# Two more zero fills with 8 KB rows while the zero buffer is half lent out

## The chip, the cores and the metric

One core of a Trainium2 chip. The metric is device time in microseconds of one execution; lower is better. A program on one core has no second state that could be seen here: all runs quoted are of the fast state, and they are compared only with runs of the kernel before from the same rounds on the same chip.

## The reference, cut to what matters

The reference is one decode step of a transformer block (attention over a window of a KV cache, then a gated FFN) with its backward pass. Only the shapes of the gradients matter:

```python
Hkv, Sk, Dh = 8, 32768, 256
W = min(4096, max(256, Sk // 4))          # 4096: only the last 4096 positions are attended to
k = jnp.repeat(k_cache[:, :, Sk - W:, :], rep, axis=1)
v = jnp.repeat(v_cache[:, :, Sk - W:, :], rep, axis=1)
# outputs 2 and 3: gradients of k_cache and v_cache, bfloat16 [1, 8, 32768, 256] each
```

Seven eighths of both cache gradients are zeros that must be written: some 235 MB out of the 281 MB that the kernel writes.

## The kernel before: the parts that matter

The zeros come from a zero buffer of 16 KB in each of the 128 partitions of SBUF, the core's on-chip memory (`ZW` = 8192 bf16 values). A **fill** writes 2.10 MB from it. Most fills use rows of 16 KB, the whole width, up to four fills in one issue. In the FFN stage SBUF is short, and the upper half of the zero buffer holds the weights of FFN block 1. Meanwhile fills are sent "in halves": rows of 8 KB, read twice from the lower half.

```python
HALF0, HALF1 = 42, 55      # fills 42..54 go out in halves
zeros = ar(0, ZW)
wgu_off = [RB + 28 * KB, ZW // 2]   # block 1's gate and up weights: upper half of the zero buffer

def send_fills(n0, n1, halves=False):
    ...
            if halves:
                for r in range(n):
                    ZQ.dma_start(out=reg[r].rearrange("p (k f) -> p k f", k=2),          # L138
                                 in_=zeros[:, 0:ZW // 2].unsqueeze(1).to_broadcast([128, 2, ZW // 2]))
            elif n == 1:
                ZQ.dma_start(out=reg[0], in_=zeros)                                      # L140
            else:
                ZQ.dma_start(out=reg.rearrange("n p f -> p n f"), in_=...)               # L142
    ...
send_fills(0, HALF0)
send_fills(HALF0, HALF1, True)
...
for n in range(len(BLOCKS)):                                    # three FFN blocks
    ...
    nc.vector.tensor_copy(out=gu_f[:, :, cs], in_=gu_ps[:, :, 0:nb])                     # L421
    ...
    for c in range(4):                                          # last use of the block's weights
        ...
        nc.vector.tensor_tensor_reduce(out=wc, in0=wc, in1=dgb[0:kp, 0:2 * w], ...)      # L438
    if n + 2 < len(BLOCKS):
        load_block(n + 2)
    if n == 1:
        nc.vector.memset(ar(ZW // 2, ZW // 2), 0.0)                                      # L443
        send_fills(HALF1, len(fills) - 1)
```

`ZQ` is GpSimd's queue; loads and other stores are issued by SyncE and ScalarE. The order of instructions on each engine, and the waits, are set by a scheduler.

## Time and profile before

| | before |
|---|---|
| median of the timed runs | 796.41 us (795.74 to 797.07) |
| busy: PE, VectorE, ScalarE | 59%, 52%, 25% of the span |
| moved by DMA | 334.75 MB, mean 420 GB/s |
| rate over 380 to 390 us | 261 GB/s |

Two lines set the scale: the table of queues (packets, MB, share of the time of the 16 DMA engines):

```profile
q0 software_dynamic: 15824, 216.01, 64.0%
q1 hardware_dynamic: 11382, 116.68, 34.9%
```

GpSimd's fills (q0) are two thirds of all bytes. They go to one queue with up to eight issues in flight, and fill every gap that the other transfers leave, as long as that queue holds something.

### The profile page before, as it was taken

Reading aid. Unit: us, or ns where it says so; the run is one execution under the profiler, and the core shown is the slowest. Engines: PE = TensorE matmul, PEld = TensorE weight load, DVE = VectorE, ACT = ScalarE, POOL = GpSimd, SP = SyncE. Lnnn points to the kernel's source line nnn. Section 1 sums busy time; section 2 is a strip of 40 time slices with the busy share of each in tenths; the row PEclk is TensorE's granted clock in tenths of the full one; section 3 lists DMA queues with packets and bytes.
Section 4 is the critical chain, followed back from the end, with each engine's and each line's share of the span. In section 5 each row is a group of like instructions: output and inputs, shape, how many; then the busy total and the mean of one; then the engine's idle time right before and its main releaser. Section 6 shows DMA issues by size and latency. Waiting matters only on the chain.

```text
span 796.7 us, 7253 instructions
## 1 busy us (share of the span) xinstructions
PE 470.7 (59%) x2926; PEld 218.9 (27%) x2926; DVE 410.4 (52%) x621; ACT 196.0 (25%) x309; POOL 35.4 (4%) x52
## 2 busy tenths in 40 slices
PE   0359998999999999353227658583450553361000
PEld 0233433344343433141116524241110211130000
DVE  2106673846648475152883488377661584472200
ACT  0043223142240301000101217372330343162200
POOL 5000000000000000100300000000000000010000
PEclk9988999999999999755557969796565556685555
DMA  9999999999999999999899999999999999999997
GB/s 349 429 431 429 429 431 430 429 430 431 429 429 430 424 425 423 416 421 422 349 421 406 429 428 428 430 431 428 426 425 432 424 429 427 427 422 410 428 443 327
DMA packets 28680, 334.75 MB, mean 420 GB/s; under 512 B 2143, under 2 KB 5223, under 8 KB 7143
## 3 DMA queue, kind: packets, MB, share of 16 engines
q0 software_dynamic: 15824, 216.01, 64.0%
q1 hardware_dynamic: 11382, 116.68, 34.9%
q10 hardware_dynamic: 1440, 1.61, 0.6%
q8 instruction: 23, 0.38, 0.2%
q14 instruction: 11, 0.08, 0.0%
HBM read 53.69 MB, written 280.59 MB: 420 GB/s over the span
## 4 chain that ended last, share of the span: by engine, by line
another core or an unknown queue 36%; DMA 29%; DVE 14%; PE 9%; issue 2%; POOL 1%; ACT 1%; DVEq 0%; ACTq 0%; SPq 0%; POOLq 0%
DMA out_dram<-arena 29%; DVE arena L469 2%; DVE arena L658 2%; DVE arena L554 2%; PE rows_ps L266 2%; PE dqb_ps L512 2%; DVE arena L659 2%; PE d_ps L651 2%; PE tr_ps L263 1%; DVE arena L524 1%; DVE arena L438 1%; POOL out_dram L138 1%; PE dqb_ps L515 1%; DVE arena L623 1%
## 5 line engine op out<-in xcount | busy, mean ns | idle before, releaser
L322 DVE TENSOR_TENSOR arena<-arena,p_f 128x2048 bf16<-128x2048 bf16 x64 | 145.3, 2286 | 64.9 <-PE M_ps L327 64.8
L327 PE MATMUL M_ps<-arena 128*128 128x512 bf16 x512 | 129.6, 382 | 0.2 <-ACT arena L333 0.2
L651 PE MATMUL d_ps<-arena 32*128 32x512 bf16 x256 | 44.8, 507 | 104.8 <-DVE arena L659 90.3
L263 PE MATMUL tr_ps<-ident_bf,arena 128*128 128x128 bf16 x1024 | 90.6, 238 | 20.0 <-DMA arena<-in_A_k_cache_dram 12.3
L266 PE MATMUL rows_ps<-arena,vpad 128*16 128x512 bf16 x256 | 87.3, 436 | 22.1 <-DVE arena L623 16.1
L263 PEld LDWEIGHTS <-arena 128*128 128x128 bf16 x1024 | 67.0, 106 | 72.8 <-issue 59.2
L280 ACT COPY arena<-tr_ps 128x1024 bf16<-128x1024 bf16 x64 | 61.8, 1016 | 69.9 <-PE tr_ps L263 69.9
L330 PE MATMUL ok_ps<-arena 128*16 128x512 bf16 x256 | 63.8, 381 | 0.9 <-DVE arena L307 0.9
L655 ACT CAST arena<-d_ps 128x512 bf16<-128x512 f32 x64 | 37.7, 588 | 103.4 <-PE d_ps L651 103.4
L327 PEld LDWEIGHTS <-arena 128*128 128x128 bf16 x512 | 43.4, 99 | 59.2 <-issue 23.5
L621 ACT COPY arena<-tr_ps 128x1024 bf16<-128x1024 bf16 x32 | 32.5, 1016 | 108.1 <-PE tr_ps L263 48.3
L659 DVE CAST arena<-d_ps 128x512 bf16<-128x512 f32 x64 | 43.5, 679 | 20.8 <-DMA out_dram<-arena 20.8
L658 DVE CAST arena<-d_ps 128x512 bf16<-128x512 f32 x64 | 43.8, 684 | 16.1 <-PE d_ps L651 15.6
L651 PEld LDWEIGHTS <-arena 32*128 32x128 bf16 x256 | 10.6, 95 | 129.9 <-issue 80.0
L656 ACT CAST arena<-d_ps 128x512 bf16<-128x512 f32 x64 | 38.2, 596 | 22.0 <-DMA out_dram<-arena 22.0
L266 PEld LDWEIGHTS <-vpad 128*16 128x16 bf16 x256 | 18.7, 91 | 57.7 <-issue 49.5
L330 PEld LDWEIGHTS <-arena 128*16 128x16 bf16 x256 | 19.1, 89 | 41.5 <-issue 20.4
L142 POOL DMA_DIRECT2D out_dram<-arena x25 | 19.3, 775 | 230.3 <-DMA out_dram<-arena 230.2
L549 DVE TENSOR_SCALAR arena<-arena,xT 128x1792 bf16<-128x1792 bf16 (+1 forms) x9 | 7.7, 881 | 35.5 <-DMA out_dram<-arena 35.5
L295 ACT ACTIVATE e_f<-cols_ps,nbias 128x32 f32<-128x32 f32 x16 | 4.5, 285 | 86.8 <-DVE nbias L291 86.8
L524 DVE CUSTOM_DVE_ANT_0 arena<-arena 128x4096 bf16<-128x4096 bf16 x3 | 13.1, 4423 | 23.2 <-ACT arena L517 23.2
L268 DVE COPY arena<-rows_ps 16x512 f32<-16x512 f32 x16 | 10.8, 676 | 27.5 <-PE rows_ps L266 27.5
(199 smaller groups left out, 388.6 us busy)
## 6 DMA issues: line engine op xcount, KB each, us to landing
out_dram<-arena POOLq DMA_DIRECT2D x13, 8192.0 KB, 167.9
out_dram<-arena POOLq DMA_DIRECT2D x12, 6144.0 KB, 171.5
out_dram<-arena SPq DMA_DIRECT2D x18, 2048.0 KB, 26.7
out_dram<-arena POOLq DMA_DIRECT2D x14, 2048.0 KB, 59.6
arena<-in_A_v_cache_dram SPq DMA_DIRECT2D x10, 2048.0 KB, 52.7
arena<-in_A_k_cache_dram SPq DMA_DIRECT2D x8, 2048.0 KB, 31.9
out_dram<-arena SPq DMA_DIRECT2D x4, 4096.0 KB, 29.9
arena<-in_A_wq_dram SPq DMA_DIRECT2D x2, 3072.0 KB, 21.3
```

The lines of the kernel that those rows point to most:

```text
L263: nc.tensor.transpose(tr_ps[:, dh, i, :], X_sb[:, 4 * q + i, dh * 128:(dh + 1) * 128], ident_bf[:])
L266: nc.tensor.matmul(rows_ps[:], lhsT=pad[:, dh, 16 * q:16 * q + 16], rhs=XT[:, dh].rearrange("p t k -> p (t k)"), start=(q == 0 and dh == 0 ...
L280: sT_ps = dots(kv_at(K_off[g]), KT_slot, vpad[g % 2], rows1, ps_c, "cols", lambda q, XT, ps: nc.scalar.copy(out=XT, in_=ps))
L322: nc.vector.tensor_tensor(out=pK, in0=K_sb[:, 4 * c:4 * c + 4, :].unsqueeze(2).to_broadcast([128, 4, 2, Dh]), in1=p_f[:, c::8, :].unsqueez ...
L327: nc.tensor.matmul(M_ps[:, vh, :], lhsT=V_sb[:, t, vh * 128:(vh + 1) * 128], rhs=pK[:, i, :, :].rearrange("p h d -> p (h d)"), start=(t == ...
L330: nc.tensor.matmul(ok_ps[:].rearrange("p k d -> p (k d)"), lhsT=ppad[g % 2][:, 8 * (t % 4) + t // 4, :], rhs=both(g, t), start=(g == 0 and ...
L621: nc.scalar.copy(out=XT, in_=ps)
L651: nc.tensor.matmul(d_ps[:, qi].rearrange("p w d -> p (w d)"), lhsT=rTm[32 * q:32 * (q + 1), l, :], rhs=R_sb[32 * q:32 * (q + 1), :], start ...
L655: nc.scalar.copy(out=stV[:, t:t + 2, :], in_=d_ps[:, :, 0, :])
L656: nc.scalar.copy(out=stK[:, t:t + 2, :], in_=d_ps[:, :, 1, :])
L658: nc.vector.tensor_copy(out=stV[:, t:t + 2, :], in_=d_ps[:, :, 0, :])
L659: nc.vector.tensor_copy(out=stK[:, t:t + 2, :], in_=d_ps[:, :, 1, :])
```

## The change

The intent: send two more fills in halves, so that GpSimd's queue holds work until the upper half of the zero buffer is zero again.

```diff
-HALF0, HALF1 = 42, 55
+HALF0, HALF1 = 42, 57
```

## The prediction

> **What bounds the kernel now.** I read four views, from coarse to fine. The page first, for the busy shares of the engines and the row of DMA rates:
>
> ```profile
> PE 470.7 (59%) x2926; PEld 218.9 (27%) x2926; DVE 410.4 (52%) x621; ACT 196.0 (25%) x309; POOL 35.4 (4%) x52
> ...
> DMA  9999999999999999999899999999999999999997
> GB/s 349 429 431 429 429 431 430 429 430 431 429 429 430 424 425 423 416 421 422 349 421 406 429 428 428 430 431 428 426 425 432 424 429 427 427 422 410 428 443 327
> ```
>
> No compute engine is above 59% of the 796.7 us, and the DMA engines are at nine tenths or more in 38 of 40 slices. 334.75 MB moved at some 428 GB/s would take 782 us by itself, so the transfers are the bound and the only time to be had is time in which they stand still. Each slice is 19.9 us. The low ones are the first (start), the last (drain) and one in the middle: slice 20, 378 to 398 us, with 349 GB/s. The second view, the windows, shows that place more finely. The columns are the stretch, its length, busy time and count of PE, PEld, DVE, ACT and POOL, the granted clock, the DMA share and GB/s:
>
> ```profile
> 364.00:380.00 16.00, 3.66 (x40) 3.19 (x40) 3.53 (x6) 0.00 (x0) 0.00 (x0) 0.50 1.02 424
> ...
> 380.00:382.00 2.00, 0.00 (x0) 0.00 (x0) 1.58 (x6) 0.00 (x0) 0.00 (x0) 0.50 0.63 262
> 382.00:384.00 2.00, 0.00 (x0) 0.00 (x0) 2.00 (x4) 0.00 (x0) 0.15 (x1) 0.50 0.11 45
> 384.00:386.00 2.00, 1.82 (x5) 0.46 (x5) 1.93 (x9) 0.00 (x0) 2.00 (x4) 0.50 0.63 270
> ...
> 380.00:390.00 10.00, 4.17 (x23) 2.53 (x24) 8.20 (x22) 1.01 (x1) 5.86 (x8) 0.50 0.67 261
> ...
> 390.00:410.00 20.00, 5.11 (x18) 3.51 (x16) 14.59 (x42) 1.51 (x4) 0.74 (x1) 0.50 1.02 431
> ```
>
> The DMA engines are nearly idle around 383 us. Over 380 to 390 us they moved 261 GB/s, where the 20 us after moved 431: (431 - 261) / 431 x 10 us = 3.9 us of lost transfer time. The third view, GpSimd in order of time, names the cause. L138 sends the fills with 8 KB rows, which read the lower half of the zero buffer alone; L140 and L142 send fills with 16 KB rows, which need both halves:
>
> ```profile
> 333.92 0.66 POOL L138 DMA_DIRECT2D out_dram<-arena  x1 [6.37 <-DMA out_dram<-arena]
> 340.11 0.67 POOL L138 DMA_DIRECT2D out_dram<-arena  x1 [5.53 <-DMA out_dram<-arena]
> 383.85 0.55 POOL L140 DMA_DIRECT2D out_dram<-arena  x1 [43.07 <-DVE arena L443]
> 384.39 5.32 POOL L142 DMA_DIRECT2D out_dram<-arena  x7
> ```
>
> The thirteenth small-row fill goes out at 340.11 us. GpSimd then stands 43.07 us, until VectorE has zeroed the upper half again (L443). Eight fills can be in flight (the issues come singly after the first eight), so at 340.11 us some eight fills of 2.10 MB were queued: 16.8 MB, or 39.6 us at 424 GB/s, ending near 380 us. That is where the rate falls. The fourth view, VectorE in order of time, says why the zeroing is not earlier:
>
> ```profile
> 376.10 0.17 DVE L421 COPY gu_f<-gu_ps 128x10 f32<-128x10 f32 x1 [13.75 <-PE gu_ps L420]
> 376.64 1.22 DVE L438 CUSTOM_DVE_ANT_0 arena<-arena 128x1024 bf16<-128x1024 bf16 x1 [0.37 <-DMA out_dram<-arena]
> ...
> 381.79 1.76 DVE L443 MEMSET arena<- 128x2048 uint32 x1 [0.41 <-DVE hh_f L424]
> ```
>
> VectorE runs its program in order, and the copy that belongs to FFN block 2 stands ahead of the last use of block 1 (L438), after which alone the upper half is free. That copy waited 13.75 us for matmuls, which waited for block 2's weights (issued at 355.7 to 357.6 us, landing up to 17.8 us later). The zeroing ends at 383.55 us. The chain of waits puts 42.70 us before L438 down to a store; I don't read that as a dependence on the last small-row fill, since L438 starts while those fills are still moving.
>
> **What the Trainium skill says.** "DMA: Bandwidth & Descriptors", section "Issuing engines are not separate DMA queues": transfers of all issuing engines run on the same 16 DMA engines and interleave. The trace agrees: fills from GpSimd and loads from SyncE together give 420 GB/s from 340 to 364 us, no more than fills alone. The same page, section "Queues, rings and completion order": each DMA engine goes round its rings packet by packet. So two fills queued behind other fills in the same ring delay no weight load, only what follows in that ring. The queue table is in keeping with long packets (216.01 MB in 15824 packets, 13.7 KB each); the turn-taking itself I can't see in it. The same page, section "Why small descriptors are slow (HBM only)", states about 3 cycles of overhead per packet and one cycle per 32 bytes. As an estimate from that page, a row of 16 KB takes 512 + 3 and two of 8 KB take 512 + 6, 0.6% more. The trace has 424 GB/s where small-row fills dominate (364 to 380 us) and 431 with 16 KB rows (390 to 410 us), 1.7% apart, so that is what I use.
>
> **The change part by part.** The order of the instructions on PE, VectorE, ScalarE and SyncE, waits included, is the same in both kernels but for buffer numbers. On GpSimd the 13 small-row issues become 15, the one single 16 KB-row fill (L140) goes and the next group of three (L142) becomes one of two. Bytes stay the same.
> - Added: two issues at 0.67 us each on GpSimd, in its 43 us wait. Cost 0. They go out as soon as two older fills have landed; the last small-row fills went out 5 to 10 us apart, so about 346 and 352 us.
> - Added to the queue: 2 x 2.10 = 4.19 MB, 9.9 us at 424 GB/s. The queue that ran dry at about 381 us now lasts to about 391 us.
> - Unmoved: the zeroing, ending at 383.55 us. Block 2's loads are in other rings, and the fill ring was full until 380 us before too, so they land as before. The 16 KB-row fills go out at 383.9 us as before, now some 7 us before the ring runs dry instead of 3 us after; their start-up lies beside the tail of the small rows.
> - Gain: 3.9 us of lost transfer time. Cost of the smaller rows: 4.19 MB at 424 instead of 431 GB/s, 9.88 - 9.72 = 0.2 us. Removed: one issue of 0.55 us, which was part of the hole already counted.
> - Sum: -3.9 + 0.2 = -3.7 us.
>
> Does it reach the end? In every 10 us window from 400 to 780 us the DMA share is 0.99 or more. GpSimd's fills end about 3.7 us sooner, SyncE's stores then have the engines to themselves sooner, and VectorE's late waits (12.05 us before 729.42) are for stores. SyncE issues its last block of stores and fills from 743.5 us on: 18.9 MB. From there to the end 20.9 MB were moved, so 2.1 MB, 4.9 us, were still queued. Even if no computation came earlier, a lead of 3.7 us fits into that queue, with 1.2 us to spare. So 796.4 - 3.7 = 792.7 us, 0.5% less.
>
> **The rivals.**
> - *The small-row fills hold up the zeroing.* L438 waits on the landing counters of all eight fill slots. If it counted the last small-row fills, two more would move it by up to 9.9 us and the hole would come back at 391 us: some 796 to 797 us, perhaps more with the FFN late. Against it: it ran at 376.64 us, and even the quickest landing of a small-row fill (45.9 us) puts the thirteenth at 386 us.
> - *The computation sets the end, and the hole was hidden.* Then nothing changes: 796 us. For it: the queue behind the last computation is only 4.9 us deep, and less than a start-up can open a new hole, of perhaps 1 us. Against it: the DMA share, and that the late computation itself waits for stores.
> - *Small rows cost more than I take.* The stretches of 412 GB/s in the FFN phase, if they were due to the fills and not to the small weight loads beside them, give 4.19 MB / 412 = 10.2 us, 0.5 us more than now: 793.1 us.
> - *A reshuffle downstream.* All stores after 384 us meet other packets; a wait can fall luckily or not by 1 to 2 us either way.
>
> **Range and chances.** The central sum is 792.7 us. The three times before spread over 1.3 us, the reshuffle gives 1 to 2 us either way, and half of the gain may be lost late: 790.8 to 795.4 us. Over 2% is 15.9 us, four times the hole, and there is no other hole of that size; a loss of that size needs a new wait in every later stage. Faster 0.01, same 0.98, slower 0.01.
>
> **What would show it.** In the profile after: fifteen L138 issues, the last near 352 us; GpSimd's wait for L443 about 12 us shorter; L443 still at about 381.8 us (right) or near 391 us (first rival right); the rate over 380 to 390 us at 420 GB/s or more instead of 261 (hole closed); the last 16 KB-row group and SyncE's last stores some 3 to 4 us earlier (lead kept), or a new low window after 690 us (second rival). I am wrong if the zeroing moves, or if the hole closes and the span stays.

## The result, and the profile after

Median 793.54 us (792.95 to 793.97, 4 runs), against 796.63 us (795.74 to 797.07, 4 runs) for the kernel before in the same rounds. Ratio 0.9962, with a 95% interval of 0.9945 to 0.9979: 3.1 us less, within 2%. (Ratios here are the mean time of one kernel's runs over that of the other's of the same rounds, so not quite the ratio of the medians quoted.)

First the page of the changed kernel, the rows of the DMA share and rate in 40 slices of 19.8 us:

```profile
DMA  9999999999999999999999999999999999999997
GB/s 346 429 431 430 429 431 430 430 430 429 432 429 427 428 426 421 415 422 421 430 434 422 424 430 429 429 424 432 426 425 429 427 426 432 432 419 407 415 435 336
```

The 349 GB/s in slice 20 is gone (430 now); only the first and last slices stay low. The same place in windows:

```profile
364.00:380.00 16.00, 3.69 (x40) 3.19 (x40) 3.62 (x8) 0.04 (x1) 0.00 (x0) 0.50 1.02 425
380.00:390.00 10.00, 4.26 (x23) 2.52 (x24) 8.11 (x22) 1.02 (x2) 4.48 (x6) 0.50 1.01 428
390.00:410.00 20.00, 5.01 (x18) 3.51 (x16) 14.67 (x42) 1.50 (x4) 1.53 (x2) 0.50 1.01 433
```

The last column is to be read: 428 GB/s over 380 to 390 us instead of 261. GpSimd in order of time shows the added issues:

```profile
340.15 0.67 POOL L138 DMA_DIRECT2D out_dram<-arena  x1 [5.49 <-DMA out_dram<-arena]
346.14 0.66 POOL L138 DMA_DIRECT2D out_dram<-arena  x1 [5.32 <-DMA out_dram<-arena]
351.85 0.67 POOL L138 DMA_DIRECT2D out_dram<-arena  x1 [5.04 <-DMA out_dram<-arena]
383.77 4.48 POOL L142 DMA_DIRECT2D out_dram<-arena  x6 [31.25 <-DVE arena L443]
```

The issues at 346.14 and 351.85 us are the two new ones, each as soon as an older fill had landed. GpSimd now waits 31.25 us for the zeroing instead of 43.07, and only six issues go out at once, because two of the eight places in flight are still taken by small-row fills: the queue has not run dry. VectorE in the same place:

```profile
376.01 0.17 DVE L421 COPY gu_f<-gu_ps 128x10 f32<-128x10 f32 x1 [13.14 <-PE gu_ps L420]
...
381.71 1.76 DVE L443 MEMSET arena<- 128x2048 uint32 x1 [0.42 <-DVE hh_f L424]
```

Nothing moved: the zeroing starts at 381.71 us, before it was 381.79. The end of the kernel, from SyncE's queue in order of time, first before, then after (L661 issues the last blocks of gradients):

```profile
715.85 7.74 SPq L661 DMA_DIRECT2D out_dram<-arena  x2
743.53 1.62 SPq L661 DMA_DIRECT2D out_dram<-arena  x2
```

```profile
719.00 3.17 SPq L661 DMA_DIRECT2D out_dram<-arena  x2
742.52 1.57 SPq L661 DMA_DIRECT2D out_dram<-arena  x2
```

The computation that feeds these stores is not 3 us earlier: one pair is 3.2 us later, the last pair 1.0 us earlier. The gain is not in the computation but in the queue of transfers. From 742.52 us on 18.87 MB were issued and, by the trace, 19.45 MB moved, so some 0.6 MB (1.3 us) was still queued at that moment, against 2.1 MB (4.9 us) before. That is 3.6 us less queue with the last stores 1.0 us earlier, and 4.6 us together: the span of this profile is 4.5 us shorter (796.7 to 792.2 us).

### The profile page after: what moved, and what is told of

It reads as the page before. It is cut to its first block, busy times and chain, and to the rows that moved or that the text cites. A ratio compares the mean times of both kernels' runs of the same rounds, so it can differ in the third digit from the quotient of the medians.

```text
span 792.2 us, 7254 instructions
## 1 busy us (share of the span) xinstructions
PE 472.8 (60%) x2926; PEld 220.0 (28%) x2926; DVE 410.6 (52%) x621; ACT 195.9 (25%) x309; POOL 36.2 (5%) x53
## 3 DMA queue, kind: packets, MB, share of 16 engines
q0 software_dynamic: 16096, 216.01, 64.1%
## 4 chain that ended last, share of the span: by engine, by line
another core or an unknown queue 36%; DMA 29%; DVE 14%; PE 9%; issue 2%; POOL 1%; ACT 1%; DVEq 0%; ACTq 0%; SPq 0%; POOLq 0%
DMA out_dram<-arena 29%; DVE arena L469 2%; DVE arena L658 2%; PE rows_ps L266 2%; DVE arena L554 2%; PE dqb_ps L512 2%; DVE arena L659 2%; PE d_ps L651 2%; PE tr_ps L263 1%; DVE arena L524 1%; DVE arena L438 1%; PE dqb_ps L515 1%; POOL out_dram L138 1%; ACT arena L621 1%
## 5 line engine op out<-in xcount | busy, mean ns | idle before, releaser
L266 PE MATMUL rows_ps<-arena,vpad 128*16 128x512 bf16 x256 | 89.0, 443 | 22.0 <-DVE arena L623 15.9
```

Source lines behind the costliest of these rows:

```text
L266: nc.tensor.matmul(rows_ps[:], lhsT=pad[:, dh, 16 * q:16 * q + 16], rhs=XT[:, dh].rearrange("p t k -> p (t k)"), start=(q == 0 and dh == 0 ...
```

## The experiments

**Theory.** The transfers alone set the end. What the change saves is one hole in them, between the last small-row fill and the zeroing, and the zeroing is late because VectorE's order puts a copy that needs block 2's weights ahead of block 1's last use. **Rivals:** the gain comes from the number of small rows; the zeroing waits for the small-row fills; the late computation sets the end, or soon will.

Eight kernels ran, in two sets of four, on two chips; each set has its own runs of the kernel before (medians 796.53 us of 11 runs and 796.83 us of 9).

### h53, h56, h57: fewer fills in halves, one more, and the change again

```diff
-HALF0, HALF1 = 42, 55
+HALF0, HALF1 = 42, 53      # h53;  42, 56 in h56;  42, 57 in h57
```

> Eleven small-row fills. Theory (the transfer hole is the whole effect): two fills of 2.10 MB less, 9.9 us at 424 GB/s, are queued when the zeroing still ends near 383 us, so the fills run dry near 371 us and the hole grows from 3.9 to some 13.7 us: 796.6 + 9.7 = 806.3 us (804.5 to 807). Rival (the end is set by computation, the hole is partly hidden): clearly less than 803 us.

> Fourteen small-row fills. Theory (hole): one more fill adds 4.9 us of queue, the fills would run dry near 386 us, after the 16 KB-row fills are issued at 383.9 us; the hole is closed but for about half a us of start-up: 793.1 to 793.8 us, the same as with fifteen. Rival (the gain goes with the number of small rows): half of the gain of fifteen, 795.1 us.

> The changed kernel again, beside the others: 793.5 us, 0.996 of before. Also a second profile of it: if the late computation near 715 us is again 1 to 3 us later than before, that lateness belongs to the change; if not, it is scatter.

| kernel | fills in halves | GB/s, 380 to 390 us | median us | ratio to before (95%) |
|---|---|---|---|---|
| h53 | 11 | 274 | 807.17 | 1.0134 (1.0115 to 1.0152) |
| before | 13 | 261 | 796.53 | 1 |
| h56 | 14 | 423 | 793.70 | 0.9967 (0.9953 to 0.9981) |
| h57 | 15 | 428 | 793.30 | 0.9961 (0.9945 to 0.9976) |

In h53 the hole starts earlier. Its windows over 364 to 380 and 380 to 390 us:

```profile
364.00:380.00 16.00, 3.65 (x40) 3.18 (x40) 4.91 (x10) 0.00 (x0) 0.00 (x0) 0.50 0.50 208
380.00:390.00 10.00, 4.97 (x25) 2.63 (x25) 7.65 (x18) 1.80 (x4) 6.12 (x8) 0.50 0.69 274
```

The engines do half their work over 16 us: (425 - 208) / 425 x 16 + (431 - 274) / 431 x 10 = 11.8 us lost. The expectation was 13.7. The zeroing ended at 381.84 us instead of 383.55, so the hole was shorter than I had taken. Of these 1.7 us, 1.3 were there already when block 2's weights were issued (354.37 us instead of 355.71); h61 and h85 below issue them as early and never run dry, so the hole is not the reason, and what is stays open. Between the two profiled executions the sum closes: the hole grew by 11.8 - 3.9 = 7.9 us and the span by 8.2 us (796.7 to 804.9). Between the medians the time rose by 10.7 us, against 9.7 expected: the profiled execution of the kernel before was a slow one (798.43 us; see the sum in "Why the prediction was right"), and the five runs of h53 spread over 3.4 us.

The response is the one of a hole, not of a count: two fills fewer cost 10.7 us, one more gains 2.8, two more gain 3.2. One fill (4.9 us of queue) covers a hole of 3.9 us; the second finds next to nothing left to cover. The rival that goes by the number of small rows expected 795.1 us for h56 and falls.

### early: the zeroing earlier, with thirteen fills in halves as before

```diff
-            nc.vector.tensor_copy(out=gu_f[:, :, cs], in_=gu_ps[:, :, 0:nb])
+            with (tc.issue_after(zeroed.ins) if n == 2 else ExitStack()):
+                nc.vector.tensor_copy(out=gu_f[:, :, cs], in_=gu_ps[:, :, 0:nb])
 ...
-                nc.vector.memset(ar(ZW // 2, ZW // 2), 0.0)
+                zeroed = nc.vector.memset(ar(ZW // 2, ZW // 2), 0.0)
```

This only queues block 2's copy behind the zeroing on VectorE. (Two other tries gave no run: a buffer of its own for block 1's weights, which did not fit, and a higher priority for L438, which left VectorE's order as it was.)

> Thirteen small-row fills as before, but block 2's first copy on VectorE is queued behind the zeroing of the upper half, so that block 1's last use and the zeroing no longer wait for block 2's weights. Theory (the late zeroing makes the hole, and it is late by VectorE's order alone): zeroing ends near 371 us instead of 383.5, the 16 KB-row fills are queued before the small ones run out, the rate over 380 to 390 us is 420 GB/s or more, and the time is 792.5 to 793.7 us without any added small row. Rival (the zeroing waits for the small-row fills, or the added rows themselves help): zeroing stays near 382 us and the time 796.6 us.

Median 793.59 us, ratio 0.9962 (0.9948 to 0.9976). VectorE's zeroing and block 2's copy (L444 and L422 in this file), GpSimd's next issue and the window, from three views of this run:

```profile
369.06 1.76 DVE L444 MEMSET arena<- 128x2048 uint32 x1 [0.49 <-DVE dhn L439]
...
376.59 0.17 DVE L422 COPY gu_f<-gu_ps 128x10 f32<-128x10 f32 x1 [5.28 <-PE gu_ps L420]
```

```profile
371.12 0.55 POOL L140 DMA_DIRECT2D out_dram<-arena  x1 [30.66 <-DMA arena<-in_B_w_gate_dram]
```

```profile
380.00:390.00 10.00, 3.42 (x23) 2.38 (x22) 8.37 (x14) 2.42 (x5) 1.54 (x2) 0.67 1.03 440
```

The zeroing ends at 370.82 us, 12.7 us sooner, and the hole is closed (440 GB/s) without one added small row. (The profile puts GpSimd's wait down to a weight load that landed about then; the issue follows the end of the zeroing by 0.30 us, as in the kernel before.) So VectorE's order made the zeroing late, and neither the small-row fills nor their count. The last stores are issued at 732.24 us, 11.3 us sooner than before, with 4.5 MB (10.5 us) still queued instead of 0.6 MB, and the time is that of the changed kernel. Computation that is 10 us ahead buys nothing.

### h61 and h85: many more fills in halves

```diff
-HALF0, HALF1 = 42, 55
+HALF0, HALF1 = 42, 61      # h61;  42, 85 in h85
```

> Nineteen small-row fills. Theory (hole): the hole is closed with fourteen, so four more than in the changed kernel gain nothing; their rows cost 8.4 MB at 424 instead of 431 GB/s, 0.3 us: 793.3 to 794.2 us. Rival (small rows help by themselves): 3 us less per two fills, below 790 us.

> Forty-three small-row fills, 28 more than in the changed kernel (58.7 MB). If the 1.7% between 424 and 431 GB/s belongs to the rows, they cost 58.7/424 - 58.7/431 = 2.2 us: 795.6 us; if only 0.6% does, 0.8 us: 794.2 us. If rings take turns by packet, loads that run beside 8 KB rows instead of 16 KB rows get more of the engines: the 3 MB weight load issued near 420 us lands in some 20 to 23 us instead of 28.6.

h61 (nineteen): median 794.20 us, ratio 0.9960 (0.9946 to 0.9975), no more gain than with fourteen. h85 (forty-three): 796.40 us, ratio 0.9989 (0.9974 to 1.0004). The difference of the two ratios, 0.0029, is 2.3 us (from the scatter of the five runs each, 1.0 to 3.4 us) for 24 more fills, 50.3 MB: in rows of 8 KB these bytes take some 2% longer than in rows of 16 KB (2.3 of 118.6 us at 424 GB/s). The 1.7% that the prediction took from two windows lies inside these bounds. That includes all else that the rows bring about. By the windows h85 falls 1.0 MB (2.3 us) behind h61 between 390 and 580 us, about where it alone still sends 8 KB rows (until some 600 us), and no further after that. Enough of them eat most of the gain.

In h85 other loads run beside 8 KB rows instead of 16 KB ones. The 3 MB load of L471, from issue to landing, first in h57, then in h85:

```profile
DMA to landing us min/median/max: 29.0/29.0/29.0
```

```profile
DMA to landing us min/median/max: 22.1/22.1/22.1
```

It lands 6.9 us sooner; in all nine kernels but h85 it takes 27.8 to 29.9 us. That is in keeping with rings (the lists of waiting transfers, one for each queue on each DMA engine) that take turns by packet ("DMA: Bandwidth & Descriptors", section "Queues, rings and completion order"), if a packet is a row. The page doesn't say that it is (it speaks of several descriptors to a packet), and no run here isolates the turn-taking. The gradients' last stores then go out much earlier:

```profile
719.21 4.12 SPq L661 DMA_DIRECT2D out_dram<-arena  x2
```

That is 23 us ahead of h57 (742.54 us), and the kernel is 2 to 3 us slower. This shows most clearly that the computation is not what is waited for.

### h57m2 and earlym2: two fills left out

Both kernels leave 4.19 MB of one output unwritten and are wrong for it (that output compares as NaN). All else stays.

```diff
-                send_fills(HALF1, len(fills) - 1)
+                send_fills(HALF1, len(fills) - 3)    # in h57 for h57m2, in early for earlym2
```

> The changed kernel with two 16 KB-row fills of the last group left out (wrong result on purpose: 4.19 MB of the output stay unwritten). If the transfers alone set the end, 4.19 MB at 430 GB/s go: 793.4 - 9.8 = 783.6 us. Rival (only some 2 us of queue are left behind the last computation, and the computation does not come earlier): 789 to 792 us, with a new low window near 735 to 745 us.

> The kernel with the early zeroing, with the same two fills left out (wrong result on purpose). Its computation runs some 10 us ahead of the changed kernel's, so both theories expect the whole 9.8 us here: 783.8 us. If it gains no more than the changed kernel without the two fills, the late computation is not what holds that one.

h57m2: median 783.47 us, ratio 0.9830 (0.9815 to 0.9844). earlym2: 783.75 us, ratio 0.9832 (0.9818 to 0.9846). Both lose the whole 9.8 us to be had for 4.19 MB. The rival, that the changed kernel has only some 2 us before the late computation binds, falls. The reason is VectorE's wait late in the kernel, in h57 and then in h57m2:

```profile
728.43 0.69 DVE L659 CAST arena<-d_ps 128x512 bf16<-128x512 f32 x1 [9.80 <-DMA out_dram<-arena]
```

```profile
719.16 0.69 DVE L659 CAST arena<-d_ps 128x512 bf16<-128x512 f32 x1 [1.73 <-DMA out_dram<-arena]
```

The wait is for a store to free a buffer. When transfers are ahead, it shrinks, and the last stores follow (733.28 us instead of 742.54). Of it 1.73 us are left, and the handover to the last stores begins to show: from 732 to 734 us the DMA share is 0.60 in h57m2. How the time goes on beyond that was not tried.

No version beats the changed kernel clearly: h56, h57, h61 and early all lie between 793.3 and 794.2 us.

## Why the prediction was right, point by point

- **The hole and its size.** Right in cause: the rate over 380 to 390 us went from 261 to 428 GB/s, and closing the hole in another way (early) gave the same time. That the estimate of the queue (16.8 MB, 39.6 us, dry near 380 us) came out right was partly luck: by the packets in the trace 14.9 MB of small rows were left to send after 340.11 us, not 16.8, and 2.5 MB of other transfers shared the engines, which together is about as long (41 us).
- **The added fills cost nothing to issue and go out near 346 and 352 us.** Measured: 346.14 and 351.85 us. GpSimd's wait was to shorten by about 12 us: 11.8.
- **The zeroing does not move.** Right, 0.08 us apart; the first rival falls.
- **The sum, -3.7 us.** Measured -3.1 us, with an interval of 1.7 to 4.4 us less. The direction and mechanism held, and 3.7 lies inside the interval. The four kernels that close the hole gain 2.6 to 3.2 us, early too, which adds no small rows, so the 0.2 us of small rows is not the term that is off. The hole was measured in one profiled execution, which took 798.43 us, above all four timed runs of before beside it (795.74 to 797.07; in the later sets 798.87 is reached). Between the two profiles the span fell by 4.5 us, between the medians by 3.1. Part of this can be seen: from 420 to 430 us that execution moved 377 GB/s, where the other kernels, h85 (391) left out, moved 410 to 426; that is some 0.9 us. That the hole, too, is smaller in a usual execution is possible, but no profile shows it. (A slip in the third rival's sum: 10.2 us in place of 9.88 gives 793.0, not 793.1.)
- **The lead reaches the end.** Right: by the bytes moved, the changed kernel is ahead of the kernel before by 1.7 MB at 390 us, 2.3 MB at 430 us and still 1.9 MB (4.4 us) at 780 us. In the details half right: GpSimd's last 16 KB-row group went out 3.2 us earlier (500.04 instead of 503.22), but SyncE's last stores only 1.0 us earlier where I had 3 to 4, and those before them 1.1 to 3.2 us later. The fallback in the same step held: most of the lead went out of the 4.9 us of queue and left 1.3. What makes the middle stores some 1 us later is open (h57 has it too: 674.46 us for the pair that stood at 673.37, and 717.14 for 715.85; h61 has it not). It costs little here.
- **The second rival, computation sets the end.** It falls three times: early and h85 compute 10 and 23 us ahead for nothing, and two fills less gave their full 9.8 us. Its warning of a new small hole came true in part: from 742 to 744 us, where the last stores begin, the DMA share is 0.83 in the changed kernel and 0.82 in h57, against 1.04 before. That is some 0.3 us.
- **Small rows.** The 1.7% taken from two windows was about right (some 2% in h85). The 0.6% estimated from the page's overhead per packet, 0.7 us for h85's 50.3 MB, lies just under the 1.0 to 3.4 us measured.

## What to carry to other kernels

Where the DMA engines are the bound, look for the slices in which they are not full, and find whose queue ran dry there; a hole is worth about its own length, and putting more in the queue than covers it buys nothing. Then ask what the refill waits for: here an instruction order on an engine far from busy held a buffer 12.7 us too long, and either a longer queue or a better order closed the same hole. A computation that ends earlier is no gain by itself when the transfers set the end, and one profiled execution measures a hole no better than the scatter of the runs.

## What the Trainium skill lacked or had wrong

- "DMA: Bandwidth & Descriptors", "Why small descriptors are slow (HBM only)": an estimate from its cycles, each row taken as one packet, gives 0.6% between rows of 16 KB and 8 KB, and it speaks of small descriptors only. These stores from SBUF to HBM lost some 2% (2.3 us, 1.0 to 3.4, for 50.3 MB more in 8 KB rows, h85 against h61).
- The same page, "SWDGE vs HWDGE vs iDMA", has packets of preferably 4096 bytes at most. The profile counts one packet for each row of 8 or 16 KB: the changed kernel has 272 packets more in GpSimd's queue (16096 against 15824), where two fills of 128 rows became 256 rows each, 256 more. (The other 16 are packets of 4 bytes, 976 instead of 960 in the trace; GpSimd makes one issue more.) Whether the profile's packet is the page's packet or one of its descriptors, no run shows.
- The same page, "Queues, rings and completion order", says that an engine goes round its rings by packet; it does not say what the row length of a background stream does to other transfers. Halving those rows brought a 3 MB load from 29.0 to 22.1 us; that turn-taking is the reason is not shown.
